# A hand-written opening order of a fused attention and gated feed-forward kernel, rewritten from the lead tiles' last scores to its end

## The chip, the cores and the metric

The kernel runs on one core of one Trainium2 chip. A core has five engines that run their own instruction queues in order and wait for each other through semaphores: TensorE (PE, matrix products into PSUM), VectorE (DVE), ScalarE (ACT), GpSimd (POOL) and SyncE (SP, which here only issues DMAs). Sixteen DMA engines move data for all queues. The metric is the device time of one execution in microseconds; the time before is the median of three runs.

## What is computed

The reference pools and projects `kv`, lets every row of `q` attend to it, and sends the result through a gated feed-forward block:

```python
kv_pool = kv.reshape(B, H // r, r, W // r, r, C).mean(axis=(2, 4))   # r = 4
k = v = kv_pool.reshape(B, -1, C) @ w_sr
s = (q @ k.transpose(0, 2, 1)) / sqrt(C)
a = exp(s - s.max(-1)); a /= a.sum(-1) + 1e-09
x = a @ v                                                            # 4 x 12288 rows, C = 128
out = (maximum(x @ w_gate, 0) * (x @ w_val)) @ w_out                 # 128 -> 1536 -> 128
```

`q` is 4 x 12288 x 128, `kv` is 4 x 384 x 32 x 128, all float32; there are 768 keys for each of the four images.

## The kernel before

The 49,152 rows are worked on in 96 tiles of 512. For a tile, PE makes scores, ACT takes exponentials, PE makes values x (transposed, in float16), and then for each of 12 blocks of 128 of the 1536 hidden columns PE makes a value block and a gate block, and adds the gated product to the output accumulator. The sums of the exponentials are not divided out before the feed-forward block; the output is scaled by the square of their inverse.

The order of instructions on every engine is written out by hand. Three lists of words hold it: `OPENING` (L75 to L99) for the start and the first six tiles, `STEADY` (L106 to L111), which is run once for every later step, and `DRAIN` (L101 to L105) and `LAST` (L100) for the end. Each word of `OPENING` is handed to `open_step` (L678), which issues the instructions of that word; each engine gets its own in the order of the words. `@n` after a word names the PSUM bank that its matrix product takes. There are eight banks of 128 x 512 float32 in the opening; two of them pair up as the `wide` tile once the first `s` word stands. A bank is free again after the copy that reads it, so a product waits for the copy of the product that held the bank before.

The words that matter here, with k the tile, n the hidden block and j a chunk of 128 keys:

- `S k.j`, `E k.j`, `V k.j` (L374, L380, L451): for the lead tiles 0 to 3, one chunk's scores on PE, their exponential on ACT, the value product on PE. `xT k` (L461) copies the finished values out of PSUM, on the engine that `ENGINES` (L66 to L74) names.
- `U ...` (L467): the sums of the lead tiles' exponentials, four products side by side; `R` (L482) transposes them on DVE, `R2` (L488) inverts and squares them, `lsc` (L493) spreads them with 16 small copies on POOL.
- `v k.n` (L502): the value block on PE. `y k.n` (L509): its copy to SBUF, on ACT (`a`) or DVE (`v`) by `ENGINES`. `g k.n` (L513): the gate block on PE. `h k.n` (L520): the gated product, on DVE, which reads the gate block from PSUM and the copy of `y`. `o k.n` (L534): its product into the output accumulator, on PE.
- `s k.i`, `e k.i` (L387, L401): a block of scores of 128 rows against all 768 keys (two products, 512 and 256 columns) and its exponential with the row sum, for tiles 4 and up. After every second `e`, SP issues a DMA transpose of the exponentials (`a_turn`, L427).
- `cast i` (L200): rows of q for tile i from float32 to float16, for tiles 4 and 5 on POOL. `qT i` (L214): for those tiles a DMA transpose on SP, which `s i` reads. `qd j` (L752) loads q for tiles 6 and 7 with POOL's queue; `tq` (L765) transposes them, with SP's queue.
- `qn k.n` (L762): POOL makes a tiny copy that reads the gated product k.n, and then issues the four loads of q for tiles 8 to 11; the copy is a gate that holds the loads back.
- `k5` (L778): a transpose of q for tiles 8 and 9 on SP and the first two loads of q for tiles 12 to 15 on POOL, into the buffer that held q of tiles 4 to 7.
- `oT k` (L776, L549): a tile's output is transposed on DVE (two buffers `o_t`), scaled on POOL, and stored with 16 DMAs, which the following `o` words issue one or two at a time. An `o` word also counts steps for `image_step` (L800), which loads the next image's `kv` a piece at a time with SP's queue.

The list ends with tile 5's scores and the gated products of tile 2; the steady list then begins with tile 6.

Of the kernel before, what the change touches and what calls it, by code (L numbers as in the profile page):

```python
# [16 lines left out]
def kernel(  # L17
# [49 lines left out]
        a0:v a1:v p0:v r0:v b1:v c1:v p1:v kvT0:v r1:p cast0:a cast1:a key0:v kvT1:v qT0:v  # L67
        cast2:a cast3:v qT1:v val0:v key1:v qT2:v qT3:v val1:a a2:v a3:v p2:p b3:v c3:v kvT2:a
        p3:p key2:a kvT3:a val2:v a5:v key3:v p5:v a4:v r5:v b4:v val3:a c4:v kvT5:a p4:v key5:v
        kvT4:a val5:v key4:v val4:v xT0:v xT2:v y0.8:v y0.2:a xT1:v y2.0:a y0.10:a cast4:p y0.7:a  # L70
        y0.6:a cast5:p y0.0:a y2.1:a xT3:a y0.1:a y1.10:a y0.5:a y0.4:a y0.3:a y0.9:a y1.8:a
        y1.1:a y1.0:a y0.11:a y1.11:v y1.3:a y2.3:a y1.7:a y1.4:a y2.2:a y2.7:a y2.4:a y1.5:a
        y1.6:a y1.2:a y2.5:v y1.9:a y2.6:a y2.11:a y2.8:a y2.9:a y2.10:a
    """.split())  # L74
    OPENING = """  # L75
        D1@2 D0@2 F384@2 a0 a1 p0 r0 T0.r@0 T0.3 b1 T0.2 c1 F256@2 p1 kvT0 r1 cast0 pj0@0 T1.r@1
# [5 lines left out]
        E3.3 V0.2 T5.2@4 E0.3 r5 T5.r vt3@7 val3 T5.3 kvT5 wo S1.3@0 S2.3@7 b4 c4 p4 V3.3 pj5@4  # L82
        V3.2 E1.3 T4.p@0 E2.3 V1.3 key5 vt5@4 S2.5@7 kvT4 val5 pj4@0 key4 E2.5 S0.5@4 E0.5 V0.3
        V2.3 S0.4@0 vt4@7 E0.4 V2.5 val4 S1.4@4 V0.5 E1.4 S2.4@7 V0.4 xT0 E2.4 S1.5@0 E1.5 S3.5@4
        V1.4 V2.4 E3.5 S3.4@7 qd3 xT2 v0.8@2 v0.2@0 E3.4 qd1 V1.5 y0.8 v0.10@4 y0.2 v2.0@1 qd0
        U2.3.4.5 xT1 y2.0 qd2 y0.10 cast4 v0.7@3 R v0.6@1 y0.7 g0.2@4 qT4 g2.0@0 h0.2 v0.0@2 y0.6
        v2.1@3 cast5 g0.7@5 h2.0 V3.5 y0.0 g0.6@4 v0.1@1 qT5 h0.7 V3.4 y2.1 v1.10@2 g0.10@0 h0.6
        xT3 o0.7@5 g0.1@3 y0.1 o0.2 h0.10 o0.6 y1.10 v0.5@4 h0.1 g0.0@1 g2.1@0 y0.5 v0.4@2 h0.0
        o0.10 y0.4 v0.3@3 g0.4@4 h2.1 o0.0 y0.3 g1.10@2 v0.9@1 h0.4 g0.5@0 y0.9 v1.8@3 h1.10 s4.0
        y1.8 o0.4 v1.1@1 h0.5 e4.0 g0.8@2 tq1 g0.9@3 h0.8 g1.8@4 v1.0@0 y1.1 o0.5 h1.8 qn1.8 s4.1  # L90
        y1.0 v1.11@2 g1.0@1 h0.9 e4.1 g0.3@4 v0.11@0 h1.0 o0.8 v1.3@3 y0.11 s4.2 y1.11 y1.3
        g1.1@1 v2.3@0 h0.3 o0.9 e4.2 g0.11@3 g2.2@2 h1.1 o0.1 y2.3 v1.7@4 o0.3 h0.11 v1.4@1 y1.7
        g1.7@0 s4.3 R2 y1.4 o0.11 h1.7 lsc e4.3 k5 g1.3@4 v2.2@1 h1.3 o1.0@3 v2.7@0 y2.2 o1.1 oT0
        o1.7 y2.7 g1.4@4 v2.4@1 h2.2 o1.3 y2.4 v1.5@0 v1.6@5 h1.4 g1.11@2 y1.5 g2.3@1 o1.8 h1.11
        y1.6 v1.2@0 g2.4@4 h2.3 s5.0 y1.2 v2.5@5 g2.6@2 h2.4 e5.0 v1.9@0 o1.10 y2.5 g2.5@1 y1.9
        g1.5@4 s5.1 h1.5 o1.4 e5.1 g1.2@0 v2.6@5 h2.5 g1.6@4 o1.11 y2.6 o1.5 h1.6 v2.11@1 s5.2
        h1.2 y2.11 o1.6 g2.7@4 e5.2 v2.8@5 h2.6 v2.9@0 g1.9@1 h2.7 o1.2 y2.8 g2.8@2 s5.3 h1.9
        y2.9 v2.10@5 g2.9@4 e5.3 h2.8 g2.11@0 o1.9 g2.10@1 h2.9 y2.10 oT1 h2.10 h2.11
    """.split()  # L99
    LAST = [f"{head}{n}" for n in range(NFB) for head in "ovygh"] + ["oT"]  # L100
    DRAIN = """  # L101
# [806 lines left out]
```

## Time and profile before

| | before |
|---|---|
| time, median of 3 runs | 1024.41 us (1024.4 to 1024.45) |
| the profiled execution's own time | 1024.25 us |
| its span, first to last instruction | 1022.5 us |
| PE busy | 1017.2 us, 99% of the span |
| ACT busy | 918.5 us, 90% |
| DVE busy | 869.4 us, 85% |
| POOL busy | 524.0 us, 51% |

The profile is that of one execution. Its page gives busy time by engine, the granted clock of PE, the DMA queues, the chain of work that ended last and the costliest groups of instructions. The trace can also be read in order of time (the timeline: start and length in us, engine, line, operation, out<-in, count, and in brackets the idle time before and what ended it), in windows with each engine's busy time, by source line, and by DMA with the time from issue to landing. Matmuls are pipelined and their ends are modelled, so the start of the next one says more than the length of one. The part of the list that changes covers some 27 to 57 us of the span.

### The profile page before, as it was taken

What the parts mean: (1) busy time and instruction counts of PE and PEld (TensorE: products, weight loads), DVE (VectorE), ACT (ScalarE), POOL (GpSimd) and SP (SyncE); (2) the same over time, 40 slices, a digit from 0 to 9 for tenths busy, and PEclk for the clock granted to TensorE, in tenths of its full rate; (3) what the DMA queues carried; (4) which work ended last, traced back from release to release, by engine and by line L of the source; (5) the groups of instructions that cost most, each with busy time, mean ns of one, the idle gap of its engine ahead of it and who ended that gap; (6) DMA issues with size and microseconds to landing.
All of it is one profiled execution on the core that took longest, in us unless ns stands there. A gap on an engine that the chain in (4) does not pass through costs nothing.

```text
span 1022.5 us, 17480 instructions
## 1 busy us (share of the span) xinstructions
PE 1017.2 (99%) x5021; PEld 485.2 (47%) x5021; DVE 869.4 (85%) x1450; ACT 918.5 (90%) x1927; POOL 524.0 (51%) x1312
## 2 busy tenths in 40 slices
PE   9999999999999999999999999999999999999998
PEld 4444444444444444444444444444444444444445
DVE  5988888888888888888888888888888888888888
ACT  5999998999999999999999999999999999999986
POOL 3487857344437576544434856754434543443342
PEclk9999999999999999999999999999999999999999
DMA  9999999878799999868779999978787878777651
GB/s 317 172 171 184 186 211 145 140 122 132 132 198 156 201 164 184 136 116 143 125 134 201 165 186 187 157 131 137 128 130 114 147 122 129 124 119 124 98 91 44
DMA packets 475743, 153.48 MB, mean 150 GB/s; under 512 B 451584, under 2 KB 465920, under 8 KB 475648
## 3 DMA queue, kind: packets, MB, share of 16 engines
q1 hardware_dynamic: 453184, 126.08, 65.9%
q0 software_dynamic: 22032, 25.19, 17.6%
q10 hardware_dynamic: 432, 1.11, 0.3%
q8 instruction: 39, 0.64, 0.3%
q14 instruction: 56, 0.46, 0.2%
HBM read 53.94 MB, written 26.35 MB: 79 GB/s over the span
## 4 chain that ended last, share of the span: by engine, by line
PE 99%; DMA 1%; DVE 0%; ACTq 0%; issue 0%
PE bank_ps L504 24%; PE bank_ps L515 24%; PE bank_ps L545 24%; PE wide_ps L397 12%; PE bank_ps L439 12%; PE bank_ps L529 1%; DMA kv_in<-in_kv_dram 1%; PE bank_ps L456 1%; PE bank_ps L378 1%; PE wide_ps L336 0%; PE bank_ps L300 0%; PE bank_ps L314 0%; PE bank_ps L474 0%; DVE kv_s L272 0%; PE bank_ps L209 0%; ACTq L246 0%
## 5 line engine op out<-in xcount | busy, mean ns | idle before, releaser
L523 DVE SCALAR_TENSOR_TENSOR hT<-bank_ps,val 128x512 f16<-128x512 f32 x1152 | 727.3, 679 | 104.4 <-PE bank_ps L515 83.7
L141 ACT CAST val<-bank_ps 128x512 f16<-128x512 f32 x1149 | 628.4, 596 | 44.4 <-PE bank_ps L504 23.9
L504 PE MATMUL bank_ps<-xT,wv 128*128 128x512 f16 x1152 | 421.0, 379 | 0.0
L515 PE MATMUL bank_ps<-xT,wg 128*128 128x512 f16 x1152 | 376.3, 379 | 0.0
L545 PE MATMUL bank_ps<-hT,wo 128*128 128x512 f16 x1116 | 348.7, 379 | 0.0
L402 ACT ACTIVATE a<-wide_ps 128x768 f16<-128x768 f32 x368 | 302.2, 821 | 44.0 <-PE wide_ps L397 44.0
L397 PE MATMUL wide_ps<-kv,qT 128*128 128x512 f16 x736 | 179.8, 326 | 0.0
L439 PE MATMUL bank_ps<-aT,kv 128*128 128x512 f16 x552 | 179.0, 379 | 0.0
L558 POOL TENSOR_TENSOR o_sb<-o_t,scale 128x512 f32<-128x512 f32 x89 | 93.2, 1047 | 158.8 <-issue 141.0
L545 PEld LDWEIGHTS <-wo 128*128 128x128 f16 x1116 | 109.1, 98 | 132.1 <-issue 0.5
L515 PEld LDWEIGHTS <-wg 128*128 128x128 f16 x1152 | 112.6, 98 | 122.5 <-issue 0.2
L504 PEld LDWEIGHTS <-wv 128*128 128x128 f16 x1152 | 112.5, 98 | 105.4 <-issue 0.4
L423 POOL COPY scale<-square 32x8 f32<-32x8 f32 x736 | 141.2, 192 | 28.6
L416 POOL TENSOR_TENSOR square<-inverse 128x8 f32<-128x8 f32 x46 | 9.3, 202 | 248.9 <-DVE inverse L414 248.9
L838 POOL DMA_DIRECT2D out_dram<-o_sb x208 | 130.3, 632 | 9.6 <-POOL o_sb L558 7.4
L397 PEld LDWEIGHTS <-qT 128*128 128x128 f16 x736 | 71.9, 98 | 87.0 <-issue 0.2
L447 DVE CAST xT<-bank_ps 128x512 f16<-128x512 f32 x92 | 63.6, 691 | 31.7 <-PE bank_ps L439 31.6
L439 PEld LDWEIGHTS <-kv 128*128 128x128 f16 x552 | 53.9, 98 | 65.2
L402 ACT ACTIVATION_READ_ACCUMULATOR a<-wide_ps 128x1 f32 x368 | 76.1, 207 | 0.0
L553 DVE STREAM_TRANSPOSE o_t<-bank_ps 128x512 f32<-128x512 f32 x93 | 65.4, 703 | 0.3 <-PE bank_ps L504 0.2
L162 POOL DMA_DIRECT2D q<-in_q_dram x84 | 48.8, 581 | 0.3 <-issue 0.3
L256 POOL TENSOR_TENSOR s<-kv_in 128x512 f32<-128x512 f32 x36 | 45.1, 1281 | 0.7
(86 smaller groups left out, 210.8 us busy)
## 6 DMA issues: line engine op xcount, KB each, us to landing
kv_in<-in_kv_dram SPq DMA_DIRECT2D x42, 512.0 KB, 5.3
out_dram<-o_sb SPq DMA_DIRECT2D x177, 64.0 KB, 3.6
q<-in_q_dram POOLq DMA_DIRECT2D x88, 128.0 KB, 3.4
out_dram<-o_sb POOLq DMA_DIRECT2D x176, 64.0 KB, 4.2
aT<-a SPq DMA_TRANSPOSE x184, 4.5
kv_line<-in_kv_dram SPq DMA_DIRECT2D x4, 512.0 KB, 9.8
placed<-blocks SPq DMA_DIRECT2D x9, 128.0 KB, 2.5
kvT<-placed SPq DMA_DIRECT2D x36, 32.0 KB, 2.2
```

The lines of the kernel that those rows point to most:

```text
L141: nc.scalar.copy(to, what)
L397: nc.tensor.matmul(s_ps[:, j0 * 128 : j1 * 128], qT, kv16[:, b, j0:j1, 0:C], start=True, stop=True)
L402: nc.scalar.activation(a16s[k][:, s, :], s_banks.pop(s)[:, 0:J], AF.Exp, scale=qk_scale, accum_out=a_sums[k // 2][:, k % 2, s : s + 1],)
L423: nc.gpsimd.tensor_copy(to[32 * b : 32 * (b + 1), :, :, j], squares[k // 2][32 * j : 32 * (j + 1)])
L439: nc.tensor.matmul(x_banks[k], kv16[:, k // NST, jc, C : 2 * C], aT[:, jc], start=first, stop=x_left[k] == 0,)
L504: nc.tensor.matmul(proj_banks["v", k, fb], wv16[:, fb * 128 : (fb + 1) * 128], xTs[k], start=True, stop=True,)
L515: nc.tensor.matmul(proj_banks["g", k, fb], wg16[:, fb * 128 : (fb + 1) * 128], xTs[k], start=True, stop=True,)
L523: nc.vector.scalar_tensor_tensor(hTs[k][:, fb, :], freed(proj_banks.pop(("g", k, fb))), 0.0, vals.pop((k, fb)), op0=ALU.max, op1=ALU.mult,)
L545: nc.tensor.matmul(o_banks[k], wo16[:, fb, :], hTs[k][:, fb, :], start=first, stop=o_left[k] == 0)
L553: nc.vector.transpose(o_t, freed(o_banks.pop(k)))
L558: nc.gpsimd.tensor_tensor(to, o_by, scale.to_broadcast([128, NS, 4, 32]), op=ALU.mult)
L838: queue.dma_start(*out_moves.pop())
```

## The change

`OPENING` is written anew from the word `E3.4` to its end: the same words in another order, some with other banks. In `ENGINES`, `xT1` and `y2.5` go from VectorE to ScalarE. Nothing else differs. On DVE this takes out two copies and makes a few groups of gated products longer; on ACT it adds them. On POOL, the cast of tile 5's q goes from ahead of the gate `qn1.8` to behind its four loads. On SP, one `kv` load goes ahead of the two transposes for tiles 4 and 5, and `tq` goes from ahead of the first two transposes of exponentials to between them.

```diff
--- before.py
+++ after.py
@@ -67,10 +67,10 @@
         a0:v a1:v p0:v r0:v b1:v c1:v p1:v kvT0:v r1:p cast0:a cast1:a key0:v kvT1:v qT0:v
         cast2:a cast3:v qT1:v val0:v key1:v qT2:v qT3:v val1:a a2:v a3:v p2:p b3:v c3:v kvT2:a
         p3:p key2:a kvT3:a val2:v a5:v key3:v p5:v a4:v r5:v b4:v val3:a c4:v kvT5:a p4:v key5:v
-        kvT4:a val5:v key4:v val4:v xT0:v xT2:v y0.8:v y0.2:a xT1:v y2.0:a y0.10:a cast4:p y0.7:a
+        kvT4:a val5:v key4:v val4:v xT0:v xT2:v y0.8:v y0.2:a xT1:a y2.0:a y0.10:a cast4:p y0.7:a
         y0.6:a cast5:p y0.0:a y2.1:a xT3:a y0.1:a y1.10:a y0.5:a y0.4:a y0.3:a y0.9:a y1.8:a
         y1.1:a y1.0:a y0.11:a y1.11:v y1.3:a y2.3:a y1.7:a y1.4:a y2.2:a y2.7:a y2.4:a y1.5:a
-        y1.6:a y1.2:a y2.5:v y1.9:a y2.6:a y2.11:a y2.8:a y2.9:a y2.10:a
+        y1.6:a y1.2:a y2.5:a y1.9:a y2.6:a y2.11:a y2.8:a y2.9:a y2.10:a
     """.split())
     OPENING = """
         D1@2 D0@2 F384@2 a0 a1 p0 r0 T0.r@0 T0.3 b1 T0.2 c1 F256@2 p1 kvT0 r1 cast0 pj0@0 T1.r@1
@@ -82,20 +82,20 @@
         E3.3 V0.2 T5.2@4 E0.3 r5 T5.r vt3@7 val3 T5.3 kvT5 wo S1.3@0 S2.3@7 b4 c4 p4 V3.3 pj5@4
         V3.2 E1.3 T4.p@0 E2.3 V1.3 key5 vt5@4 S2.5@7 kvT4 val5 pj4@0 key4 E2.5 S0.5@4 E0.5 V0.3
         V2.3 S0.4@0 vt4@7 E0.4 V2.5 val4 S1.4@4 V0.5 E1.4 S2.4@7 V0.4 xT0 E2.4 S1.5@0 E1.5 S3.5@4
-        V1.4 V2.4 E3.5 S3.4@7 qd3 xT2 v0.8@2 v0.2@0 E3.4 qd1 V1.5 y0.8 v0.10@4 y0.2 v2.0@1 qd0
-        U2.3.4.5 xT1 y2.0 qd2 y0.10 cast4 v0.7@3 R v0.6@1 y0.7 g0.2@4 qT4 g2.0@0 h0.2 v0.0@2 y0.6
-        v2.1@3 cast5 g0.7@5 h2.0 V3.5 y0.0 g0.6@4 v0.1@1 qT5 h0.7 V3.4 y2.1 v1.10@2 g0.10@0 h0.6
-        xT3 o0.7@5 g0.1@3 y0.1 o0.2 h0.10 o0.6 y1.10 v0.5@4 h0.1 g0.0@1 g2.1@0 y0.5 v0.4@2 h0.0
-        o0.10 y0.4 v0.3@3 g0.4@4 h2.1 o0.0 y0.3 g1.10@2 v0.9@1 h0.4 g0.5@0 y0.9 v1.8@3 h1.10 s4.0
-        y1.8 o0.4 v1.1@1 h0.5 e4.0 g0.8@2 tq1 g0.9@3 h0.8 g1.8@4 v1.0@0 y1.1 o0.5 h1.8 qn1.8 s4.1
-        y1.0 v1.11@2 g1.0@1 h0.9 e4.1 g0.3@4 v0.11@0 h1.0 o0.8 v1.3@3 y0.11 s4.2 y1.11 y1.3
-        g1.1@1 v2.3@0 h0.3 o0.9 e4.2 g0.11@3 g2.2@2 h1.1 o0.1 y2.3 v1.7@4 o0.3 h0.11 v1.4@1 y1.7
-        g1.7@0 s4.3 R2 y1.4 o0.11 h1.7 lsc e4.3 k5 g1.3@4 v2.2@1 h1.3 o1.0@3 v2.7@0 y2.2 o1.1 oT0
-        o1.7 y2.7 g1.4@4 v2.4@1 h2.2 o1.3 y2.4 v1.5@0 v1.6@5 h1.4 g1.11@2 y1.5 g2.3@1 o1.8 h1.11
-        y1.6 v1.2@0 g2.4@4 h2.3 s5.0 y1.2 v2.5@5 g2.6@2 h2.4 e5.0 v1.9@0 o1.10 y2.5 g2.5@1 y1.9
-        g1.5@4 s5.1 h1.5 o1.4 e5.1 g1.2@0 v2.6@5 h2.5 g1.6@4 o1.11 y2.6 o1.5 h1.6 v2.11@1 s5.2
-        h1.2 y2.11 o1.6 g2.7@4 e5.2 v2.8@5 h2.6 v2.9@0 g1.9@1 h2.7 o1.2 y2.8 g2.8@2 s5.3 h1.9
-        y2.9 v2.10@5 g2.9@4 e5.3 h2.8 g2.11@0 o1.9 g2.10@1 h2.9 y2.10 oT1 h2.10 h2.11
+        V1.4 V2.4 E3.5 S3.4@7 E3.4 v0.8@2 v0.10@0 y0.10 V1.5 v0.2@4 y0.2 qd3 xT2 qd1 qd0 v2.0@1
+        y2.0 xT1 U2.3.4.5 v0.0@4 y0.8 y0.0 v0.7@0 y0.7 g0.2@1 qd2 g2.0@2 cast4 R h0.2 V3.5 v0.1@5
+        g0.10@4 g0.1@3 h2.0 v0.6@1 h0.10 g0.7@0 h0.7 y0.1 V3.4 y0.6 h0.1 v2.1@5 v0.5@2 o0.2@4
+        g0.0@1 h0.0 o0.10 xT3 o0.7 y2.1 v1.10@0 g0.6@5 h0.6 y0.5 y1.10 g1.10@3 qT4 v0.3@2 o0.1
+        g0.5@1 h1.10 y0.3 v0.9@0 y0.9 o0.6 v1.8@2 y1.8 h0.5 g0.9@5 h0.9 v0.4@3 y0.4 g2.1@0 s4.0
+        h2.1 g0.8@2 g1.8@1 h1.8 qn1.8 o0.5 v1.0@3 v1.1@5 v0.11@0 e4.0 h0.8 y1.0 s4.1 g0.4@1 y0.11
+        g0.3@3 cast5 o0.0 g0.11@0 h0.4 qT5 h0.3 y1.1 e4.1 o0.8 v1.3@5 y1.3 h0.11 v1.11@1 y1.11
+        o0.4 v1.7@2 y1.7 s4.2 e4.2 g1.7@3 h1.7 g1.0@0 h1.0 v2.3@5 v1.4@2 y2.3 v2.7@1 y1.4 o0.3
+        g1.3@3 h1.3 o0.11 o0.9 g1.4@0 tq1 y2.7 v2.2@5 h1.4 R2 lsc g1.1@2 h1.1 y2.2 v2.4@3 g1.11@1
+        y2.4 s4.3 o1.3@5 e4.3 k5 o1.4 v1.6@3 h1.11 y1.6 g2.2@0 v1.5@2 y1.5 o1.10 s5.0 g2.3@1 h2.2
+        oT0 e5.0 g1.5@3 o1.8 v2.6@2 h1.5 y2.6 g1.6@0 h1.6 v2.5@4 y2.5 o1.0 s5.1 g2.6@2 e5.1
+        v2.11@3 v1.9@4 o1.1 g2.7@0 h2.3 h2.6 v1.2@1 y2.11 y1.9 h2.7 s5.2 y1.2 g2.4@2 h2.4 o1.11
+        g2.5@3 v2.10@4 v2.8@0 e5.2 g1.2@1 g1.9@2 o1.7 y2.8 h2.5 o1.5 h1.2 h1.9 s5.3 y2.10 g2.11@3
+        h2.11 e5.3 g2.10@1 h2.10 g2.9@0 v2.9@4 y2.9 o1.6 g2.8@2 h2.8 o1.9 o1.2 h2.9 oT1
     """.split()
     LAST = [f"{head}{n}" for n in range(NFB) for head in "ovygh"] + ["oT"]
     DRAIN = """
```

## The prediction

> **What bounds the kernel now.** The page first: its first line, the row of busy times, the granted clock and the chain of work that ended last.
>
> ```profile
> span 1022.5 us, 17480 instructions
> PE 1017.2 (99%) x5021; PEld 485.2 (47%) x5021; DVE 869.4 (85%) x1450; ACT 918.5 (90%) x1927; POOL 524.0 (51%) x1312
> PEclk9999999999999999999999999999999999999999
> PE 99%; DMA 1%; DVE 0%; ACTq 0%; issue 0%
> ```
>
> PE ends the span and is busy in 99% of it at full clock. Busy PE is modelled, so I did not take it as proof of a packed PE; I counted starts in the timeline of PE instead. In that view each row is a start, a length and a line; L397 is a score block, two matmuls.
>
> ```profile
> 30.34 0.59 PE L515 MATMUL bank_ps<-xT,wg 128*128 128x512 f16 x2
> ...
> 36.17 0.49 PE L397 MATMUL wide_ps<-kv,qT 128*128 128x512 f16 x2
> 36.50 0.38 PE L545 MATMUL bank_ps<-hT,wo 128*128 128x512 f16 x1
> 36.71 0.38 PE L504 MATMUL bank_ps<-xT,wv 128*128 128x512 f16 x1
> ...
> 46.15 0.49 PE L397 MATMUL wide_ps<-kv,qT 128*128 128x512 f16 x2
> ...
> 52.71 0.38 PE L515 MATMUL bank_ps<-xT,wg 128*128 128x512 f16 x1
> 53.00 0.38 PE L504 MATMUL bank_ps<-xT,wv 128*128 128x512 f16 x1
> 53.22 0.49 PE L397 MATMUL wide_ps<-kv,qT 128*128 128x512 f16 x2
> 53.60 0.38 PE L545 MATMUL bank_ps<-hT,wo 128*128 128x512 f16 x1
> ...
> 63.64 0.49 PE L397 MATMUL wide_ps<-kv,qT 128*128 128x512 f16 x2
> ...
> 986.68 0.49 PE L397 MATMUL wide_ps<-kv,qT 128*128 128x512 f16 x2
> ```
>
> A 512-column matmul holds PE for 0.216 us (36.50 to 36.71) and a score block for 0.325 (36.17 to 36.50, after rounding). The rows at 30.34, 36.17, 46.15, 53.22 and 63.64 are the list's words g0.2, s4.0, s5.0 and the first score blocks of tiles 6 and 7. Counting matmul words between them in the old list and the steady list:
> - g0.2 to s4.0: 27 matmuls, 5.83 us of work in 5.83 us.
> - s4.0 to s5.0: 40 matmuls and 4 score blocks, 9.94 in 9.98: idle 0.04.
> - s5.0 to tile 6: 26 and 4, 6.92 in 7.07: idle 0.15. The two largest waits are visible: 52.71 to 53.00 (0.08 too long) and 53.22 to 53.60 (0.06).
> - tile 6 to tile 7: 42 and 4, 10.37 in 10.42: idle 0.05.
>
> After that, 986.68 is the fourth score block of tile 95, which lies 27 matmuls and 3 blocks (6.81 us) behind its first; so 88 tiles took 916.2 us, 10.41 each against 10.37 of counted work. **PE is packed**, and all that this stretch can give back is 0.24 us. The windows between those starts say who stands close behind PE (busy us and counts of PE, PEld, DVE, ACT, POOL, then clock, DMA share, GB/s).
>
> ```profile
> 28.60:36.20 7.60, 7.60 (x48) 3.21 (x47) 7.17 (x13) 7.10 (x15) 1.22 (x2) 1.00 0.77 138
> 36.20:46.20 10.00, 10.00 (x50) 4.70 (x49) 9.97 (x20) 9.97 (x22) 5.29 (x21) 1.00 0.98 162
> 46.20:53.20 7.00, 7.00 (x35) 3.25 (x34) 6.94 (x12) 6.65 (x16) 6.29 (x12) 1.00 1.22 214
> 53.20:63.60 10.40, 10.40 (x51) 4.88 (x50) 9.08 (x16) 9.64 (x21) 8.66 (x19) 1.00 1.08 193
> ```
>
> DVE and ACT are both nearly full, and the DMA engines are full from 36 us on.
>
> **The change part by part.** *The order itself.* Both lists hold the same 111 matmul words from V1.4 on, so PE's work is the same: 0 us. s4.0 has 37 single matmuls and the sums ahead of it in both, and stays at 36.17. s5.0 moves forward: 35 matmuls and 4 blocks (8.86 us) lie between them instead of 40 and 4, so it is due at 45.03, 1.1 earlier. Tile 6 stays at 53.1.
>
> *The copies xT1 and y2.5, from DVE to ACT.* DVE and ACT rows:
>
> ```profile
> 30.02 0.72 DVE L486 STREAM_TRANSPOSE sums_turned<-bank_ps 128x512 f32<-128x512 f32 x1 [0.40 <-PE bank_ps L474]
> 30.75 9.08 DVE L523 SCALAR_TENSOR_TENSOR hT<-bank_ps,val 128x512 f16<-128x512 f32 x15
> ...
> 47.31 0.67 DVE L143 CAST val<-bank_ps 128x512 f16<-128x512 f32 x1
> ...
> 57.00 2.48 DVE L523 SCALAR_TENSOR_TENSOR hT<-bank_ps,val 128x512 f16<-128x512 f32 x4 [0.93 <-PE bank_ps L515]
> ```
>
> ```profile
> 36.90 0.83 ACT L402 ACTIVATE a<-wide_ps 128x768 f16<-128x768 f32 x1
> ...
> 37.70 1.08 ACT L141 CAST val<-bank_ps 128x512 f16<-128x512 f32 x2
> ...
> 43.44 3.42 ACT L141 CAST val<-bank_ps 128x512 f16<-128x512 f32 x6
> ```
>
> A DVE step costs (9.08 - 0.68) / 14 = 0.60 us. xT1's stands ahead of the sums' transpose, which waits for PE for 0.40 anyway: its removal gives 0. y2.5 is the copy at 47.31, and after it DVE runs without a gap until its 0.93 of idle before 57.00; 0.60 less there covers waits of 0.08 and 0.06 and the rest of that stage. Bounds of the gain: 0 (each wait reappears behind another word) and 0.24 (all idle goes). I take **-0.15**, the idle of the one stage that y2.5 stands in. For ACT I count from s4.0 to tile 6, 16.9 us: 20 copies instead of 19 and 8 exponentials. An exponential takes 0.80 (36.90 to 37.70), a copy 0.48 where two follow each other (1.08 less a last one of 0.60): 20 x 0.48 + 8 x 0.80 = 16.0, so it fits and costs 0. Its other bound is a rival below.
>
> *cast5 and with it qT5.* This is the move with a price. The queues of POOL and SP:
>
> ```profile
> 31.91 0.61 POOL L143 CAST q<-q_late 128x512 f16<-128x512 f32 x1 [1.09 <-DMA q_late<-in_q_dram]
> 38.70 0.19 POOL L763 CAST gate<-hT 128x1 f32<-128x1 f16 x1 [6.18 <-DVE hT L523]
> 39.24 2.18 POOL L162 DMA_DIRECT2D q<-in_q_dram  x4 [0.35 <-issue]
> ```
>
> ```profile
> 30.85 2.89 SPq L216 DMA_TRANSPOSE qT<-q  x2
> 33.84 0.56 SPq L246 DMA_DIRECT2D kv_in<-in_kv_dram  x1
> 39.61 1.47 SPq L429 DMA_TRANSPOSE aT<-a  x1
> 41.13 1.34 SPq L246 DMA_DIRECT2D kv_in<-in_kv_dram  x1
> ```
>
> The last column of the landing lines is issue to landing: of L216, of L766, and of the page's and the 38 to 46 us window's aT transposes, with the two queues' shares in that window.
>
> ```profile
> DMA to landing us min/median/max: 2.4/2.5/2.5
> DMA to landing us min/median/max: 5.1/5.1/5.1
> aT<-a SPq DMA_TRANSPOSE x184, 4.5
> aT<-a SPq DMA_TRANSPOSE x2, 7.3
> kv_in<-in_kv_dram SPq DMA_DIRECT2D x1, 512.0 KB, 8.7
> q1 hardware_dynamic: 2123, 0.57, 51.2%
> q0 software_dynamic: 482, 0.44, 46.3%
> ```
>
> Before, cast5 ran at 31.91, its transpose had landed by about 35, and s5.0 read it at 46.15. Now cast5 stands on POOL behind the gate, which waits for h1.8, and four q loads. h1.8 is the 12th gated product after the sums' transpose instead of the 13th, so the gate opens at 38.70 - 0.60 = 38.1; gate to the end of the four issues is 2.72 (38.70 to 41.42), the cast 0.61: 41.4. The transpose lands 2.5 later, **43.9 to 44.0, with 1.1 us left** before s5.0 at 45.03. Cost 0, and the cover is thin. From above: the nearest row under load is the aT transpose that ran beside these same q loads, 7.3 where 4.5 is usual. Stretched by that ratio qT5 takes 4.05 and is 0.45 late; with the same 2.8 added it takes 5.3 and is 1.7 late. I take 0, because in the new order the aT transpose and the kv_in load no longer share the engines with the q loads when qT5 comes, and by then the loads have had 2.7 us alone.
>
> The Trainium skill (DMA: Bandwidth & Descriptors, "Queues, rings and completion order") says that each DMA engine goes round robin between its rings, a packet at a time. The shares of q1 and q0 in the window, 51.2% and 46.3%, agree with it. If q loads were outstanding all through qT5, that rule would double its 2.5 (estimate): landing at 46.4, 1.4 late, a sum of +1.25 instead of -0.15. That is the first rival.
>
> *The rest of SP's and POOL's queues.* On SP, one kv_in load goes ahead of qT4, and qT5, aT (tile 4), kv_in now stand ahead of tq1. qT4: even if it lands 2.8 later than its 2.5 (30.85 + 5.3 = 36.15), s4.0 at 36.17 has it: 0. tq1: after 41.4 come SP issues of 1.45 (half of 2.89), 1.47 and 1.34, so it issues at 45.7 and lands at 50.8 by its own 5.1, 54.4 by the 8.7 of the kv_in load beside it; tile 6 reads it at 53.1. Cost 0 by the first, 1.3 by the second; I take 0, its own row. On POOL the next two q loads wait for tq1's landing, and behind them stands the scaling of the first output tile, some 4 us later than before. Who waits is DVE's third output transpose (two buffers), due about 59.5, so 7 us of cover: 0. The aT of tile 4 is read after tile 6 starts: covered too.
>
> Sum: 0 - 0.15 + 0 + 0 = -0.15 on the profiled execution's 1024.25 (span 1022.5 and 1.75 around it): 1024.10. The median of the runs, 1024.41, is 0.16 above that execution, so **1024.26**.
>
> **Rivals.**
> - *qT5 late.* s5.0 waits at the head of PE's in-order queue and everything behind it shifts; PE has no idle to make it up. For it: two rings sharing engines, 7.3 against 4.5. Against it: the q loads' head start. Price 0.45 to 1.7, so 1024.7 to 1026.0, middle 1025.3, and slower than before from a landing of about 3.8 us after issue on. tq1 late (1.3, 1025.6) falls in the same span and is not added, since a late s5.0 puts tile 6 off too. If qT5 takes all of the 7.3 that the aT transpose took, it is 3.7 late: 1028.0; from a landing of 5.9 us on the loss is over 0.2%. This is the case on the other side.
> - *ACT becomes the bound.* Six copies in a row took (3.42 - 0.60) / 5 = 0.56 each. At that pace its share is 20 x 0.56 + 6.4 = 17.6 us in 16.9, and PE waits 0.7 for banks: 1025.0. Against it: the pairs at 0.48 show that 0.56 is a pace set by PE.
> - *The waits only change place*, for PE still catches DVE up: 1024.41.
> - *A gain over the bound* would need 2 us out of 0.24 us of idle; only something after tile 7 that I don't see could give it.
>
> **How the numbers follow.** 0.2% of 1024.4 is 2.05 us; less than that a measurement of this kernel can hardly tell from no change. Forecast 0.50; qT5 or tq1 late by less than 2 us 0.18, qT5 late by more 0.10; ACT 0.12; change of place 0.08; a gain over 2 us 0.02. So faster 0.02, same 0.88, slower 0.10. All but the 0.12 at the two ends lie between 1024.0 (all 0.24 idle gone, less 0.1 of scatter) and 1026.0; I take 1023.9 to 1025.9. The likeliest case alone spans 1024.0 to 1024.5.
>
> **What would show it.** In the changed profile s4.0 stands at 36.2, s5.0 at 45.0 and tile 6 at 53.1 with no PE start over 0.1 late between them; L763 near 38.1, cast5 near 40.9, the second L216 near 41.4 landing before 44.9; DVE without y2.5 and ACT without idle over 1 us. Wrong would be: a gap in PE right before s5.0 or tile 6 with the DMA of qT as its releaser; PE starts after long gaps behind ACT's copies; or a difference in the time that is not in the stretch from 28 to 64 us.

## The result and the profile after

The changed kernel takes 1026.11 us (median of 17 runs, 1025.3 to 1028.51); the kernel before, beside it, 1024.41 (17 runs, 1024.2 to 1024.82). The ratio is 1.002, with a 95% interval of 1.0013 to 1.0026: slower by 1.7 us, and with runs spread over 3.2 us instead of 0.6. That is past the upper end of the range (1025.9), and slower where a gain of 0.15 was forecast.

The profiled execution took 1027.49 us. Its page, same rows as before:

```profile
span 1025.7 us, 17480 instructions
PE 1017.5 (99%) x5021; PEld 485.5 (47%) x5021; DVE 868.5 (85%) x1448; ACT 920.1 (90%) x1929; POOL 524.9 (51%) x1312
PEclk9999999999999999999999999999999999999999
PE 94%; DMA 4%; issue 1%; POOL 1%; SPq 0%; ACTq 0%; DVE 0%; POOLq 0%
```

PE is busy for 0.3 us more and the span is 3.2 us longer, so PE stood idle; in the chain of waits DMA has 4% where it had 1% (3% of the span is 31 us: the chain runs along transfers, and its share is not the size of the holes). The timeline of PE has two holes, each with a DMA as releaser:

```profile
36.23 0.49 PE L397 MATMUL wide_ps<-kv,qT 128*128 128x512 f16 x2
...
44.99 0.38 PE L545 MATMUL bank_ps<-hT,wo 128*128 128x512 f16 x1
46.71 0.50 PE L397 MATMUL wide_ps<-kv,qT 128*128 128x512 f16 x2 [1.34 <-DMA qT<-q]
...
54.71 0.49 PE L397 MATMUL wide_ps<-kv,qT 128*128 128x512 f16 x2
...
112.69 0.38 PE L504 MATMUL bank_ps<-xT,wv 128*128 128x512 f16 x1
114.69 0.38 PE L439 MATMUL bank_ps<-aT,kv 128*128 128x512 f16 x1 [1.62 <-DMA aT<-a]
```

s5.0 was due at 44.99 + 0.216 = 45.21 and starts at 46.71: **1.50 us**. At 114.69 a value product is 2.00 - 0.216 = **1.78 us** late. Together 3.28, and 1024.25 + 3.28 = 1027.53: the two holes are the whole difference of the two profiled executions (1027.49). POOL, the row of L216 for qT5 alone, and from the waits between 28 and 120 us (total, times, longest) POOL's wait for tq and the waits of PE and of its weight loads (PEld) for a DMA:

```profile
38.13 0.19 POOL L763 CAST gate<-hT 128x1 f32<-128x1 f16 x1 [7.75 <-DVE hT L523]
38.66 2.18 POOL L162 DMA_DIRECT2D q<-in_q_dram  x4 [0.35 <-issue]
40.83 0.63 POOL L143 CAST q<-q_late 128x512 f16<-128x512 f32 x1
...
51.75 1.08 POOL L162 DMA_DIRECT2D q<-in_q_dram  x2 [4.03 <-DMA qT<-q]
```

```profile
L216 SPq DMA_TRANSPOSE qT<-q x1: 1190/1190/1190, 41.5 to 41.5; - x1
...
DMA to landing us min/median/max: 5.2/5.2/5.2
```

```profile
POOL q L162 <- DMA qT<-q: 4.0, 1, 4.0
...
PEld L397 <- DMA qT<-q: 1.8, 1, 1.8
PE bank_ps L439 <- DMA aT<-a: 1.6, 1, 1.6
...
PE wide_ps L397 <- DMA qT<-q: 1.3, 1, 1.3
```

The gate, the cast and the issue of qT5 stand where the prediction put them (38.1, 40.9, 41.4). The landing does not: 5.2 us after the issue instead of 2.5. And POOL, which then waits 4.0 us for tq, was worked out and held to be covered.

### The profile page after: what moved, and what is told of

Its sections match the earlier page's. It is cut to its first block, busy times and chain, and to the rows that moved or that the text cites. A ratio compares the mean times of both kernels' runs of the same rounds, so it can differ in the third digit from the quotient of the medians.

```text
span 1025.7 us, 17480 instructions
## 1 busy us (share of the span) xinstructions
PE 1017.5 (99%) x5021; PEld 485.5 (47%) x5021; DVE 868.5 (85%) x1448; ACT 920.1 (90%) x1929; POOL 524.9 (51%) x1312
## 3 DMA queue, kind: packets, MB, share of 16 engines
q10 hardware_dynamic: 432, 1.11, 0.3%
## 4 chain that ended last, share of the span: by engine, by line
PE 94%; DMA 4%; issue 1%; POOL 1%; SPq 0%; ACTq 0%; DVE 0%; POOLq 0%
PE bank_ps L515 24%; PE bank_ps L504 23%; PE bank_ps L545 23%; PE bank_ps L439 12%; PE wide_ps L397 11%; DMA aT<-a 1%; DMA kv_line<-in_kv_dram 1%; PE bank_ps L529 1%; DMA kv_in<-in_kv_dram 1%; DMA q_late<-in_q_dram 1%; DMA qT<-q 1%; PE wide_ps L336 0%; POOL q L162 0%; POOL q L143 0%; SPq L192 0%
```

## The experiments

Three theories were set against each other. Theory 1: qT5 lands late because cast5 is late, and s5.0 waits. Theory 2: tq is late, POOL waits for it, and POOL's lag makes later transposes of exponentials late. Theory 3: two more copies make ACT the bound. Each kernel ran beside the kernel before, whose median in these series was 1024.20 (27 to 33 runs in each; beside experiment 7 it ran once, 1024.17).

**1. cast5 early.**

```diff
-        y2.0 xT1 U2.3.4.5 ... g2.0@2 cast4 R h0.2
+        y2.0 xT1 U2.3.4.5 ... g2.0@2 cast4 cast5 R h0.2
-        g0.3@3 cast5 o0.0
+        g0.3@3 o0.0
```

> The changed kernel with cast5 back ahead of the gate on POOL; nothing else. Theory 1 (qT5 late): its transpose is issued near 31.5 us instead of 41.5 and has landed long before the fifth score block; the 1.5 us gap there is gone, and the median falls from 1026.1 by at least 1.4, to 1024.7 or less, by all of 1.7 if the later gap at 114.7 us is only its echo. Theory 2 (tq late, which holds POOL and by that the later loads and transposes): tq issues about 1 us earlier only, POOL still idles 2 to 4 us for it, and some runs stay over 1025.5. Theory 3 (ACT as the bound after two more copies): no change, 1026.1.

Median 1024.20, level with before; but 4 of 11 runs took 1025.51 to 1027.91. Its profiled execution (1024.11) has no wait of PE for a DMA up to 120 us, and POOL still waits for tq:

```profile
POOL q L162 <- DMA qT<-q: 3.8, 1, 3.8
```

**2. tq early.** To let tq read before qT5 does, its buffer is dropped from the table at `k5` instead of at `tq`.

```diff
-        h0.6 y0.5 y1.10 g1.10@3 qT4 v0.3@2
+        h0.6 y0.5 y1.10 g1.10@3 qT4 tq1 v0.3@2
-        g1.4@0 tq1 y2.7
+        g1.4@0 y2.7
```

> The changed kernel with tq right behind the first of the two q transposes on SP; cast5 stays late. Theory 1: the gap before the fifth score block stays at 1.3 to 1.6 us, the median at 1025.5 to 1025.9. Theory 2: POOL's 4 us of idle time before its next two q loads is gone, the gap near 114.7 us as well, and the spread of the runs shrinks from 3.2 us to under 1. If theory 2 alone were the cause the median would fall to 1024.4.

Median 1025.31, and all 11 runs within 1025.14 to 1025.44. s5.0 still waits, POOL no longer does:

```profile
46.45 0.50 PE L397 MATMUL wide_ps<-kv,qT 128*128 128x512 f16 x2 [1.05 <-DMA qT<-q]
```

```profile
47.68 1.08 POOL L162 DMA_DIRECT2D q<-in_q_dram  x2
```

So each theory owns its half: the late cast gives a steady loss, the late tq the spread. (With cast5 early the late tq does not move the median, 1024.20; with cast5 late it does, 1026.11 against 1025.31. Why it weighs more there was not tried.)

**3 and 4. Both early, and once more.** The two edits above together.

> Both of the above together. Theories 1 and 2 together: what is left of the change is its order and the two copies, 1024.1 to 1024.4 with a spread under 0.6 us, which is level with or 0.1 to 0.3 under the kernel before. Theory 3: still 1025 or more, with PE starts late behind ACT's copies.

> The changed kernel with cast5 and tq early once more, beside the kernel before on the same chip, to see whether it is faster than before: its matmuls took 0.09 us less from the 60th to the last in one profile each. Expected 0.05 to 0.15 us under the kernel before, if that is more than chance.

Medians 1024.11 and 1024.22, beside 1024.20 and 1024.20; one of 11 runs in each was over 1025. s5.0 starts at its due place:

```profile
44.80 0.38 PE L545 MATMUL bank_ps<-hT,wo 128*128 128x512 f16 x1
45.02 0.49 PE L397 MATMUL wide_ps<-kv,qT 128*128 128x512 f16 x2
```

All of the loss is gone, theory 3 has nothing left to explain, and nothing that can be measured is won.

**5. The old order with cast5 and qT5 late.**

```diff
-        U2.3.4.5 ... v2.1@3 cast5 g0.7@5 ... v0.1@1 qT5 h0.7
+        U2.3.4.5 ... v2.1@3 g0.7@5 ... v0.1@1 h0.7
-        o0.5 h1.8 qn1.8 s4.1
+        o0.5 h1.8 qn1.8 cast5 qT5 s4.1
```

The buffer is dropped at `k5`, as in experiment 2.

> The kernel before with only cast5 and the transpose qT5 put behind the gate and its four loads. Theory 1: the cast ends near 42.0 us, the transpose lands 5.2 us after its issue as in the changed kernel, near 47.3, and the fifth score block, due at 46.15, waits 1.1 us: 1025.4 to 1025.7. If the transpose takes only its 2.5 us of a quiet queue it lands at 44.6 and the time stays at 1024.4. Theory 3: 1024.4.

1024.89, 0.69 over before. The transpose, issued at 42.0, landed 4.8 us later, and s5.0, due a microsecond later in this order than in the new one, waited less:

```profile
46.87 0.50 PE L397 MATMUL wide_ps<-kv,qT 128*128 128x512 f16 x2 [0.63 <-DMA qT<-q]
```

One cast put behind four loads makes the old order slower too: theory 1 holds without the rest of the change. The size expected was 1.1.

**6. The loads away from the late transpose.** `gt` is a new word: the gate's copy without its loads.

```diff
-        h1.8 qn1.8 o0.5
+        h1.8 o0.5
-        g0.3@3 cast5 o0.0 g0.11@0 h0.4 qT5 h0.3 y1.1 e4.1
+        g0.3@3 o0.0 g0.11@0 h0.4 h0.3 gt0.3 gt0.3 gt0.3 cast5 qT5 y1.1 e4.1
-        o1.3@5 e4.3 k5
+        o1.3@5 e4.3 qn1.8 k5
```

> The changed kernel with the four q loads put off until after the fourth exponential of tile 4, and cast5 held at its late place by three gate copies, so that qT5 is issued near 41.3 us as in the changed kernel, first on SP as there, but with no q load in flight. If the q loads stretch the transpose (5.2 us in the changed kernel, 4.9 in the one with tq early), it now lands within 2.4 to 3.0 us, before 44.5, and the fifth score block does not wait. If a transpose at this time takes 5 us for another reason, the gap of 1 to 1.5 us stays. The time itself may be raised by the loads' lateness elsewhere (tile 8's transposes).

qT5 was issued at 41.1, and s5.0 did not wait:

```profile
L216 SPq DMA_TRANSPOSE qT<-q x1: 1190/1190/1190, 41.1 to 41.1; - x1
...
DMA to landing us min/median/max: 2.4/2.4/2.4
```

2.4 us here, 4.9, 4.8 and 5.2 in the three kernels with the loads (experiments 2 and 5, and the changed one). The hour alone is not the cause, nor is SP's next transpose: it follows 1.3 us behind qT5 in all four. But the loads are not the only thing that was absent. The DMA view of the changed kernel from 44.4 us, when the last load was landing, to 46.7 has one packet of a queue that it calls instruction, taken here as instruction fetch (packets, MB, share of 16 engines):

```profile
q1 hardware_dynamic: 945, 0.24, 130.8%
q8 instruction: 1, 0.02, 2.5%
```

2.5% of 16 engines' 2.3 us is 0.9 us of one engine. Such a packet began while qT5 was in flight in all three kernels with the long landing (at 44.0, 44.3 and 44.6), and at 43.4, when qT5 had landed, in this one. Experiment 7 parts the two.

The time itself rose to 1027.8 (median of five runs), by another way. SP waited 6.7 us for the put-off loads with the transpose of `k5` (issued at 56.40 instead of 50.72), the transposes of exponentials behind it in SP's order were late in turn (the next was issued at 59.61 instead of 54.91), and values waited for exponentials, as at 71.76 for 1.76 us.

**7. The fetch without the loads.** As in 6, with eight `gt0.3` instead of three, one execution.

```diff
-        h0.3 gt0.3 gt0.3 gt0.3 cast5 qT5
+        h0.3 gt0.3 gt0.3 gt0.3 gt0.3 gt0.3 gt0.3 gt0.3 gt0.3 cast5 qT5
```

> The kernel with the q loads put off, with eight gate copies instead of three ahead of cast5, so that qT5 is issued near 42.3 us. In the kernel with three, the one packet of instruction fetch began at 43.4, when qT5 (41.1 to 43.5) had just landed; in all three kernels where qT5 took 4.8 to 5.2 us such a fetch began while it was in flight (44.0 to 44.6). Now the fetch should fall into qT5's flight with no q load there. If the loads alone stretch the transpose, it lands 2.4 to 2.8 us after its issue. If the fetch holds up one of the engines, and the transpose with it, it takes 3.6 us or more, and the fifth score block waits.

qT5 was issued at 42.5 and the fetch began at 43.5; no q load was under way.

```profile
DMA to landing us min/median/max: 3.9/3.9/3.9
```

```profile
46.44 0.50 PE L397 MATMUL wide_ps<-kv,qT 128*128 128x512 f16 x2 [1.12 <-DMA qT<-q]
```

So the fetch is a cause of its own: 2.4 without either, 3.9 with the fetch alone (+1.5, one execution), 4.8 to 5.2 with both (another 0.9 to 1.3). No kernel here has the loads without the fetch, so that the two simply add up is not shown. In this order the loads come still later, and one value product waited 7.3 us for its exponentials; the one time was 1035.85.

**8. Only tq late, in the old order.**

```diff
-        g0.8@2 tq1 g0.9@3
+        g0.8@2 g0.9@3
-        h1.7 lsc e4.3 k5
+        h1.7 lsc tq1 e4.3 k5
```

> The kernel before with only tq put behind the first pair of tile 4's exponentials, their transpose and one kv load on SP. Theory 2: POOL idles for it ahead of the next two q loads by 2 to 4 us; the median stays at 1024.2, but 2 to 5 of 11 runs are over 1025.2, as 4 of 11 were with cast5 early and tq late (1025.5 to 1027.9). If tq's place is harmless in itself, at most 1 of 11, as before (1 of 33).

Median 1024.35, five of 11 runs more than 0.5 over the fastest, up to 1025.62. The profiled execution (1025.30) shows the late hole alone:

```profile
111.22 0.38 PE L504 MATMUL bank_ps<-xT,wv 128*128 128x512 f16 x1
112.50 0.38 PE L439 MATMUL bank_ps<-aT,kv 128*128 128x512 f16 x1 [0.90 <-DMA aT<-a]
```

**9 and 10. POOL late by idle work, tq early, in the old order.** `lsc` twice, then three times; the copies write the same values again.

```diff
-        h1.7 lsc e4.3 k5
+        h1.7 lsc lsc e4.3 k5
```

> The kernel before with the 16 small copies of the lead tiles' scales done twice, which makes POOL 3.7 us late at the place where it idles for tq in the changed kernel, with tq at its early place. Theory 2 in the form 'POOL's lag makes the later loads collide with the transposes of exponentials near 100 to 115 us': a tail as with tq late, 2 to 5 of 11 runs over 1025.2. If the tail comes from tq's own lateness or from SP's order, at most 1 of 11.

> The kernel before with the 16 small copies of the scales done three times: POOL 7.5 us late from 46 us on, cast5 and tq early. Theory 2 by POOL's lag: more runs than with 3.7 us (2 of 11 more than 1 us over the fastest) wait for a transpose of exponentials, 4 or more of 11 over the fastest by 0.5 us, and the profile shows loads landing late near 100 to 115 us. If POOL's lag does nothing, 0 to 1 of 11.

Medians 1024.68 and 1025.74; runs more than 0.5 over the fastest: 3 and 8 of 11. With the copies three times, PE waits in two places:

```profile
70.67 0.39 PE L439 MATMUL bank_ps<-aT,kv 128*128 128x512 f16 x1 [0.48 <-DMA aT<-a]
...
112.61 0.38 PE L439 MATMUL bank_ps<-aT,kv 128*128 128x512 f16 x1 [0.31 <-DMA aT<-a]
```

So a lag of POOL is enough, whatever makes it. Ordered by when POOL issues the two loads behind `lsc` (one profiled execution each; experiments 6 and 7, which move the loads themselves, are left out):

| kernel | two loads issued at, us | runs over the fastest by more than 0.5 us |
|---|---|---|
| before | 46.25 | 5 of 105 |
| before, copies on ACT (12) | 46.73 | 1 of 11 |
| both early | 47.46 and 47.63 | 2 of 22 |
| before, cast5 late (5) | 47.49 | 3 of 11 |
| tq early | 47.68 | 0 of 11 |
| both early, copies on DVE (11) | 47.71 | 0 of 11 |
| before, scales twice | 50.60 | 3 of 11 |
| before, tq late | 51.25 | 5 of 11 |
| cast5 early | 51.38 | 4 of 11 |
| changed | 51.75 | 12 of 17 |
| before, scales three times | 54.42 | 8 of 11 |

Up to 47.71 it is 11 of 171 runs, from 50.60 on 32 of 61. The order within the two groups is not strict, so the time of issue is not all of it. With the scales twice, the fastest run is already 0.4 over before, and its profile has no hole in PE for that; this part is not explained.

**11 and 12. The copies by themselves.** Both early with the copies back on DVE, and the old order with the copies on ACT.

```diff
-        ... xT1:a ... y2.5:a
+        ... xT1:v ... y2.5:v
```

> The changed kernel with cast5 and tq early (1024.11) and the two copies xT1 and y2.5 back on DVE. My step: y2.5 on DVE costs PE up to 0.15 us of waits, so 1024.2 to 1024.35. Rival (ACT near its bound): the copies cost ACT as much as they free on DVE, 1024.0 to 1024.1.

> The kernel before with only the copies xT1 and y2.5 moved from DVE to ACT. My step says -0.15 (bounds 0 and -0.24): 1024.0 to 1024.1 beside 1024.2. In the new order with cast5 and tq early the two copies were worth 0.43 (1024.54 with them on DVE, 1024.11 on ACT); if they are worth as much in the old order the median is 1023.8, more than all the idle time that I counted there. Rival (ACT near its bound): 1024.2 to 1024.6.

In the new order the copies on DVE cost 0.43 (1024.54 against 1024.11; against the second series, 1024.22, it is 0.32); PE waits for DVE's backlog:

```profile
47.65 0.38 PE L504 MATMUL bank_ps<-xT,wv 128*128 128x512 f16 x1
48.28 0.38 PE L504 MATMUL bank_ps<-xT,wv 128*128 128x512 f16 x1 [0.25 <-DVE val L143]
```

In the old order the copies on ACT cost 0.86 (1025.06), against my step. PE then comes late around xT1 and y2.5, the second time with ACT as the releaser; two of the places:

```profile
29.77 0.72 PE L504 MATMUL bank_ps<-xT,wv 128*128 128x512 f16 x2
30.60 0.59 PE L515 MATMUL bank_ps<-xT,wg 128*128 128x512 f16 x2
```

```profile
48.58 0.38 PE L545 MATMUL bank_ps<-hT,wo 128*128 128x512 f16 x1
49.16 0.38 PE L515 MATMUL bank_ps<-xT,wg 128*128 128x512 f16 x1 [0.20 <-ACT val L141]
```

The gate block after 29.77 starts 0.83 behind two products that take 0.43; the one after 48.58 is 0.58 behind one of 0.22. The assignment fits one order and not the other.

## Why the prediction was wrong

- *What bounds it.* Right. PE was packed, had 0.24 us to give, and every hole in it is a loss: the two holes add up to the difference.
- *The order itself, 0 us; s5.0 due at 45.03, 1.1 earlier.* Right (45.02 with both early).
- *The copies, -0.15.* Order and copies together with both transposes early are worth -0.09 and +0.02, so not distinguishable from 0 and inside the bounds. As a price of the copies alone it was wrong: -0.32 to -0.43 in the new order, +0.86 in the old. I took DVE's relief from a count of work, and that count does not say which word waits.
- *cast5 and qT5, taken as 0: the step that failed.* The chain up to the issue was right to 0.1 us, and both ends of the landing stood in the text. I took the quiet end, 2.5, because "by then the loads have had 2.7 us alone". That head start did not end them: the last landed at 44.6, 3.1 us after qT5 was issued. The landing of qT5 took 5.2, close to the upper bound of 5.3, and s5.0 waited 1.50 us in the profiled execution. By medians, each against its own before, this is +1.20 (tq early +1.11, both early -0.09). Half of the reason is one that the prediction did not have: an instruction fetch in the same microseconds, 1.5 of the 2.7 us by experiment 7 (one execution); if the two add up, about 1.2 is left for the loads. The rule of the Trainium skill that the prediction cited ("DMA: Bandwidth & Descriptors", "Queues, rings and completion order") gave 5.0 by the estimate there. The size fits, but the loads were not outstanding all through qT5 and are not the only company, so these runs neither bear it out nor speak against it.
- *tq, taken as 0.* Tile 6 did not wait for it (54.71 is 1.5 later than 53.22 before, the size of the first hole). Right for PE.
- *POOL behind tq, "7 us of cover: 0": the second step that failed.* I asked who waits for POOL and found only DVE. I did not ask where POOL's later DMAs go. Landing rows between about 86 and 106 us, four q loads and then three transposes of exponentials, first of the changed kernel, then of before:

```profile
DMA to landing us min/median/max: 3.5/8.5/9.5
DMA to landing us min/median/max: 6.1/10.9/12.6
```

```profile
DMA to landing us min/median/max: 5.1/5.4/6.5
DMA to landing us min/median/max: 5.8/5.8/7.4
```

The late loads fall on the transposes, and both take longer. PE waits for the transpose of 10.9, issued at 103.70; the one of 12.6, issued at 97.17, kept nothing waiting. The landing is not all: in experiment 8, where PE runs level with before up to the hole, the same transpose was issued 2.4 us later than before (104.07 against 101.66) and landed in 8.3 instead of 5.8. SP's in-order queue also carries output stores that POOL scales first, which may be the reason for the late issue. That POOL's lag brings the lateness about is shown by experiments 9 and 10; by which of these transfers was not tried. By medians the late tq costs 0.59 on top (1.70 less 1.11), with cast5 late; with cast5 early it is 0.09 (1024.20 in experiment 1, 1024.11 with both early).
- *The rivals.* "qT5 late" was named, with 0.45 to 1.7 as its price and the releaser to look for, and got 0.28 in all. ACT as the bound did not occur in the new order.

## What to carry to other kernels

When a transfer is moved later, its landing has to be taken from rows with the same company on the DMA engines, not from its own quiet row: here 2.4 us became 5, with plain loads and an instruction fetch beside it. A packed engine has no idle time that could absorb the delay, so the loaded bound belongs in the forecast and the quiet one in the rival. An engine that is off the path and comes late is not checked by who waits for its results alone; its DMAs come late too, and by them the bound engine can stall 60 us further on, in some runs and not in others. And when a transfer is put off, the queue that waits for it in order puts off everything behind it (experiment 6).

## What the hardware showed beyond that

One packet of instruction fetch can hold up a whole DMA transpose. In the changed kernel the last of the four loads was issued at 40.3 and the slowest took 4.3 us, so they had landed by 44.6; qT5 landed at 46.7. In half-microsecond windows (busy times, clock, DMA share, GB/s):

```profile
44.50:45.00 0.50, 0.50 (x4) 0.19 (x2) 0.50 (x2) 0.50 (x3) 0.41 (x3) 1.00 4.09 214
45.00:45.50 0.50, 0.37 (x2) 0.00 (x0) 0.50 (x2) 0.50 (x4) 0.42 (x3) 1.00 0.49 42
45.50:46.00 0.50, 0.00 (x0) 0.00 (x0) 0.50 (x2) 0.50 (x2) 0.42 (x3) 1.00 0.41 12
```

The share counts a packet whole in the window in which it begins. So 4.09 does not mean busy engines there, nor 0.49 and 0.41 quiet ones: the packets that began between 44.5 and 45.0 lasted 2.0 us for each of the 16 engines (4.09 x 0.5), long past that window. The DMA view of 44.8 to 45.0 us has most of that time:

```profile
q1 hardware_dynamic: 88, 0.02, 842.0%
```

In the trace's records of single packets, most packets of the transposes take 0.018 us; 22 that began between 44.8 and 45.6 took 0.8 to 1.5 us, and all of these end between 46.35 and 46.40. Of the 16 signals that make up qT5's landing, 14 come between 46.35 and 46.66. The fetch begins at 44.63 and takes 0.92 us. In experiment 7 it is 12 packets of 0.9 to 1.2 us, which end together at 45.48 behind a fetch from 43.45 to 44.66; in experiment 6 no packet took over 0.06 us while qT5 was in flight.

How the fetch acts was not tried: a transpose whose last packets are queued behind the fetch on one of the 16 engines, while the others hold theirs until it has caught up, would look like this. The records name neither the engine of a packet nor the transpose that it belongs to.
